# Wave 0's v loaded by GpSimd with the cast on the way, instead of by SyncE in float32

## The chip, the core and the metric

The kernel runs on one core of a Trainium2 chip. The core has a matrix engine (TensorE, "PE" in the profile), a vector engine (VectorE, "DVE"), a scalar engine (ScalarE, "ACT"), a general engine (GpSimd, "POOL") and a queue engine (SyncE, "SP"). Each runs its own instructions in order, and they wait for one another by semaphores. Transfers from and to device memory (DMAs) are issued by SP, ACT or POOL and carried out by 16 DMA engines that all of them share. The metric is the time of the whole program in device microseconds. Before the change it is 216.82 us, the median of 3 runs (216.48 to 217.40).

## What is computed

Two layers follow each other. The first is a linear attention with a decay per head, over 4 batches, 8 heads, 768 positions and 64 channels, block by block:

```python
intra = einsum('bhic,bhjc->bhij', qb, kb) * Dmask[None]
intra = einsum('bhij,bhjd->bhid', intra, vb)
inter = einsum('bhid,bhde->bhie', qb * lam_pow[None], kv_state)
out[:, :, sl] = intra + inter
kv_state = lam_block[None, :, None, None] * kv_state + einsum('bhsd,bhse->bhde', kb * rev_pow[None], vb)
```

Its result, seen as 3072 tokens of 512 channels, goes through an MLP with 2048 hidden units:

```python
h = x @ w_in
g = h * (1.0 / (1.0 + np.exp(-1.702 * h)))
return (g @ w_out).astype(np.float32)
```

All inputs and the output are float32; the kernel multiplies in bfloat16.

## The kernel before

The 768 positions are cut into 6 waves of 128 positions. A wave is all 4 batches and all 8 heads of its positions, so 512 tokens. The heads go in 4 pairs. For each wave and pair there is a tile of k, one of q and one of v, each of 128 positions x 4 batches x 2 heads x 64 channels. `load` (L78) fetches a tile by two DMAs, one for each head (L90), all from SP's queue; each moves 128 KB in 512 pieces of 256 bytes, since 64 float32 channels are all that lies together in memory.

The attention of a wave and pair goes through these steps. `cast_k` and `cast_q` (L176, L183) scale k and q by powers of the decay and write them as bfloat16. `cast_v` (L195) copies v as bfloat16 into `v_sb`, which holds for each batch the two heads with a block of zeros between them: [v of head 0, zeros, v of head 1]. `step_a` (L205) transposes k and q on TensorE, and VectorE copies the result out (L212). `step_s` (L220) multiplies k by q (L226), and VectorE applies the decay mask (L229, `sm`). `step_c` (L268) multiplies the masked scores by v (L280), and ScalarE writes the tokens `xT` (L283). `step_kv` (L233) makes the state for the next wave (L239), which in wave 0 ScalarE copies into `kv_sb` (L244).

The MLP of a wave follows: `mlp1` (L286) makes 16 chunks of hidden units from 4 chunks of tokens, ScalarE applies the activation (L296), and `mlp2` (L313) gives 4 output tiles. The order of instructions is written by hand. In wave 0, with which the program starts, the loop of L376 runs over the pairs, with filler matmuls (`keep_warm`, L328) between the steps, and the MLP of wave 0 begins when three pairs are done. From then on the attention of the next wave is woven into the MLP of this one.

SP's queue at the start holds, in this order, k and q of pairs 0 and 1, v of pair 0, k and q of pair 2, v of pair 1, k and q of pair 3, v of pair 2, then the first weight chunk `w_first` (512 KB, float32, L76), then v of pair 3. SP then waits for a weight chunk of `w_out` (L156), so that wave 1's loads stay behind the weights.

GpSimd sets up the identity, the index columns and the mask, clears the middle blocks of wave 0's `v_sb` (L367) and the first states (L369), casts v of pairs 0 and 1, and then waits for the last q (`pool_behind_loads`, L160) before it issues the weights of L144: `w_in_160`, `w_in_161`, `w_in_162`. These DMAs turn float32 into bfloat16 on the way. Behind them it casts the first half of `w_first` (L399), casts v of pair 3, and issues `w_in_163` and the four chunks of `w_out` (L149). ScalarE casts v of pair 2 and the other half of `w_first` (L400). The matmuls of the MLP start with that first chunk (`w_in_159` in the profile).

Of the kernel before, what the change touches and what calls it, by code (L numbers as in the profile page):

```python
# [24 lines left out]
def kernel(  # L25
# [13 lines left out]
    nc = tc.nc  # L39
# [3 lines left out]
    P = 128  # L43
    NP = H // 2
# [27 lines left out]
    loaded = {}  # L72

    def load_w_first():
        f = moe_w_in.rearrange("(kc ki) f -> ki kc f", ki=P)[:, :, 0 : IN_COLS[0] * P]
        nc.sync.dma_start(out=w_first, in_=f)  # L76

    def load(w, pairs=None, names="kqv"):  # L78

        if pairs is not None:  # L80
            order = [(nm, p) for p in pairs for nm in names]
        else:
            order = [x for p in range(NP) for x in [("k", p), ("q", p), ("v", p - 1)] if x[1] >= 0] + [("v", NP - 1)]
        for nm, p in order:
            if (w, nm, p) == (0, "v", NP - 1):
                load_w_first()
            x = ld.tile([P, B, 2, D], f32, tag=f"{nm}{p}", name=f"{nm}f")
            src = {"k": k, "q": q, "v": v}[nm]
            for h in range(2):
                nc.sync.dma_start(  # L90
                    out=x[:, :, h, :],
                    in_=src[:, 2 * p + h, w * P : (w + 1) * P, :].rearrange("b s d -> s b d"))
            loaded[nm, w, p] = x

# [39 lines left out]
    v_sb = [[const.tile([P, G, 3, D], bf16, name=f"v_sb{i}{p}") for p in range(NP)] for i in range(2)]  # L136
# [5 lines left out]
    def load_w_in(j):  # L142
        f0 = sum(IN_COLS[:j]) * P
        nc.gpsimd.dma_start(  # L144
            out=w_in_sb[j], in_=moe_w_in.rearrange("(kc ki) f -> ki kc f", ki=P)[:, :, f0 : f0 + IN_COLS[j] * P])

    def load_w_out():
        for j, x in enumerate(w_out_sb):
            nc.gpsimd.dma_start(  # L149
                out=x, in_=moe_w_out.rearrange("(fc fi) d -> fi fc d", fi=P)[:, j * CW : (j + 1) * CW, :])  # L150
# [3 lines left out]
    def sync_behind_weights():  # L154

        nc.sync.dma_start(out=behind, in_=w_out_sb[1][0:1, 0, 0:2])  # L156
# [3 lines left out]
    def pool_behind_loads():  # L160

        nc.gpsimd.tensor_copy(behind_q, loaded["q", 0, NP - 1][0:1, 0, 1, 0:1])
# [13 lines left out]
    def cast_k(w, p):  # L176
        kqs_of[w, p] = work.tile([P, 2, B, 2, D], bf16, tag=f"kqs{p}", name="kqs")
        f = loaded.pop(("k", w, p))
        for h in range(2):
            eng = (nc.gpsimd, nc.scalar)[h] if w == 1 else nc.vector  # L180
            scaled(eng, kqs_of[w, p], 0, f, p, h, k_pow)

    def cast_q(w, p):  # L183
        f = loaded.pop(("q", w, p))
        for h in range(2):
            eng = nc.scalar if w < 2 and not (w == 0 and p == NP - 1 and h == 1) else nc.vector
            scaled(eng, kqs_of[w, p], 1, f, p, h, q_pow)
        cast[w, p] = kqs_of[w, p].rearrange("p i b h d -> p i b (h d)")
        if w > 1:
            kq = work.tile([P, 2, B, P], bf16, tag=f"kq{p}", name="kqT")  # L190
            nc.sync.dma_start_transpose(out=kq.rearrange("p i b s -> p (i b) s"),
                                        in_=kqs_of[w, p].rearrange("p i b h d -> p (i b h d)"))
            trans[w, p] = kq

    def cast_v(w, p):  # L195
        copy = nc.scalar.copy if (w, p) == (0, NP - 2) else nc.gpsimd.tensor_copy
        copy(v_sb[w % 2][p][:, :, 0:3:2, :], loaded.pop(("v", w, p)))

    def do_cast(w, p):
        cast_k(w, p)  # L200
# [4 lines left out]
    def step_a(w, p):  # L205
        ps_t = ps.tile([P, 2, B, P], bf16, tag="s", bufs=4, name="ps_t")
        for i in range(2):
            for b in range(B):
                nc.tensor.transpose(ps_t[:, i, b, :], cast[w, p][:, i, b, :], ident)  # L209
        kq = work.tile([P, 2, B, P], bf16, tag=f"kq{p}", name="kq")  # L210
        for i in range(2):
            nc.vector.tensor_copy(kq[:, i], ps_t[:, i])  # L212
        trans[w, p] = kq
# [114 lines left out]
    def keep_warm(n):  # L328

        for _ in range(n):  # L330
            nc.tensor.matmul(warm_ps, ident, ident.rearrange("p (o s) -> p o s", o=1).to_broadcast([P, B, P]),  # L331
                             start=True, stop=True)
# [30 lines left out]
        return [(i - (14 if w == 2 else 20), x) for i, x in zip(at, steps)]  # L363

    with tc.manual_schedule():
        for p in range(NP):
            nc.gpsimd.memset(v_sb[0][p][:, :, 1, :], 0.0)  # L367
        for p in range(NP):
            nc.gpsimd.memset(kv_sb[1][p], 0.0)  # L369
        keep_warm(10)  # L370
        cast_k(0, 0)
        cast_q(0, 0)

        nc.scalar.activation(warm, q_pow[:, 0:1], GELU)
        step_a(0, 0)
        for p in range(1, NP):  # L376
            if p == NP - 1:
                pool_behind_loads()
                load_w_in(1)
                load_w_in(2)  # L380
                load_w_in(3)
            cast_k(0, p)
            cast_q(0, p)
            cast_v(0, p - 1)
            if p < NP - 1:
                keep_warm(2)
                step_s(0, p - 1)
                keep_warm(2)
                step_a(0, p)
                step_c(0, p - 1)  # L390
                step_kv(0, p - 1)
        p = NP - 1
        keep_warm(2)
        step_s(0, p - 1)
        keep_warm(2)
        step_a(0, p)
        keep_warm(2)
        step_c(0, p - 1)
        nc.gpsimd.tensor_copy(w_in_sb[0][:, :, 0:P], w_first[:, :, 0:P])  # L399
        nc.scalar.copy(w_in_sb[0][:, :, P : 2 * P], w_first[:, :, P : 2 * P])  # L400
        step_s(0, p)
        step_kv(0, p - 1)
        keep_warm(3)
        cast_v(0, NP - 1)
        load_w_in(4)
        load_w_out()
        sync_behind_weights()
        load(1)
        side, main = [(EARLY - 1, (step_c, 0, NP - 1)), (2 * EARLY, (step_kv, 0, NP - 1))], []
        for i in range(NP):  # L410
            side += [(4, (nc.gpsimd.memset, v_sb[1][i][:, :, 1, :], 0.0)), (4, (nc.gpsimd.memset, kv_sb[0][i], 0.0))]
        for w in range(NW):
            n = len(main)
            main += mlp_items(w)
            e = len(main)
            if w + 1 < NW:
                if w == 0:
                    m = EARLY + FFC
                    for at, f, p in ((9, cast_k, 0), (9, cast_q, 0), (11, step_a, 0), (11, cast_k, 1), (11, cast_q, 1),
                                     (11, cast_v, 0), (12, step_s, 0), (13, step_a, 1), (13, cast_k, 2),  # L420
                                     (13, cast_q, 2), (13, cast_v, 1), (14, step_kv, 0), (14, step_c, 0),
                                     (14, step_s, 1), (15, step_a, 2), (15, cast_k, 3), (15, cast_q, 3),
                                     (15, cast_v, 2), (15, cast_v, 3), (15, step_kv, 1), (15, step_c, 1),
                                     (15, step_s, 2), (16, step_a, 3), (16, step_kv, 2), (16, step_c, 2),
                                     (16, step_s, 3), (16 + EARLY - 1, step_c, 3), (16 + 2 * EARLY, step_kv, 3)):
                        side += [(m + at, (f, 1, p))]
                else:
                    for p in range(NP):
                        side += [(n + 1 + 2.0 * p, (do_cast, w + 1, p))]
                        if w == 1 and p < 2:  # L430
                            side += [(n + 1 + 2.0 * p, (load, 2, [p + 2], "kq"))]
                        elif w == 1:
                            side += [(n - 1 + 2.0 * p, (load, 2, [2 * p - 4, 2 * p - 3], "v"))]
                            side += [(n + 7 + p, (cast_v, 2, i)) for i in (2 * p - 4, 2 * p - 3)]
                    side += [(e + i, s) for i, s in attn_steps(w + 1)]
            if w == 0:
                side += [(EARLY + FFC + 3 * (FFC // CW), (load, 2, [0, 1], "kq"))]
            elif w + 2 < NW:
                side += [(n + 8 + 3 * p, (load, w + 2, [p])) for p in range(NP)]
        side.sort(key=lambda x: x[0])  # L440
        for i, (f, *a) in enumerate(main):
            while side and side[0][0] <= i:
                _, (g, *b) = side.pop(0)
                g(*b)
            f(*a)
# [30 lines left out]
```

## Time and profile before

| What | Value |
|---|---|
| Median of 3 runs | 216.82 us (216.48 to 217.40) |
| The profiled execution's own time | 216.82 us |
| Its span, first to last instruction | 215.1 us |
| TensorE busy | 206.1 us (96%) |
| VectorE, ScalarE, GpSimd busy | 89.6, 89.0, 33.4 us |
| TensorE clock granted | 0.997 |
| First MLP matmul starts | 19.99 us |

The profile is of one execution. Its times count from the first instruction; 1.7 us of the measured time lie outside the span. "SPq" and "POOLq" are instructions that only issue a DMA; the transfer itself shows as the time from issue to landing. "PEld" is TensorE's weight load, which runs beside the matmuls. An entry such as "19.99 1.47 PE L293 MATMUL ... x6 [0.75 <-POOL w_in_159 L399]" means: six matmuls of line 293 begin at 19.99 us and fill 1.47 us, and before them the engine sat idle for 0.75 us until GpSimd had written `w_in_159`. The buffers of `v_sb` for wave 0 are `v_sb_143` to `v_sb_146`, those of `kv_sb` for wave 1 `kv_155` to `kv_158`.

### The profile page before, as it was taken

How to read it: one execution, taken by the hardware profiler on the slowest of the kernel's cores; microseconds unless marked ns; L12 is line 12 of the kernel's file. 1: busy time of each engine (PE TensorE's matmuls, PEld its weight loads, DVE VectorE, ACT ScalarE, POOL GpSimd, SP SyncE). 2: the span in 40 equal slices, each digit the busy share in tenths (PEclk: the TensorE clock that was granted, in tenths of full speed). 3: DMA queues.
4: the chain of work that ended last, by engine and by line, in shares of the span. 5: the costliest groups of instructions: out<-in, count | busy, mean ns of one | idle time of the engine just before them, and what ended most of it. 6: DMA issues, size and time to landing. Idle time of an engine off the chain costs nothing.

```text
span 215.1 us, 3747 instructions
## 1 busy us (share of the span) xinstructions
PE 206.1 (96%) x1435; PEld 105.1 (49%) x1435; DVE 89.6 (42%) x193; ACT 89.0 (41%) x160; POOL 33.4 (16%) x65
## 2 busy tenths in 40 slices
PE   7687999999899999999999999999999999999993
PEld 2344444457544465545555445555445545444453
DVE  0775000079835348575173655274645061100121
ACT  5674864265277221166511176411266411466000
POOL 7126910234000222140111000121000000000000
PEclk9999999999999999999999999999999999999998
DMA  5999999999999999999899499899393114100112
GB/s 125 221 222 234 201 207 206 213 223 265 226 211 197 182 205 225 224 278 199 184 216 223 151 167 203 180 182 249 118 173 50 24 52 138 57 0 0 52 49 98
DMA packets 108117, 35.64 MB, mean 166 GB/s; under 512 B 100164, under 2 KB 105156, under 8 KB 108100
## 3 DMA queue, kind: packets, MB, share of 16 engines
q1 hardware_dynamic: 103732, 31.47, 69.5%
q0 software_dynamic: 4224, 3.93, 11.3%
q8 instruction: 11, 0.18, 0.4%
q14 instruction: 6, 0.05, 0.1%
q10 hardware_dynamic: 144, 0.00, 0.0%
HBM read 27.27 MB, written 6.29 MB: 156 GB/s over the span
## 4 chain that ended last, share of the span: by engine, by line
PE 85%; SPq 5%; DVE 4%; DMA 3%; issue 1%; POOL 0%; DVEq 0%
PE ps_h L293 38%; PE ps_out L318 36%; SPq L90 5%; DMA w_first<-in_moe_w_in_dram 3%; PE ps_s L226 2%; DVE sm L229 2%; PE ps_out L305 2%; PE ps_kv L239 2%; PE ps_o L260 1%; PE ps_o L280 1%; PE ps_o L258 1%; PE ps_o L278 0%; DVE kv_151 L246 0%; DVE kv_152 L246 0%; PE ps_t L209 0%
## 5 line engine op out<-in xcount | busy, mean ns | idle before, releaser
L296 ACT ACTIVATE g_sb<-ps_h 128x512 bf16<-128x512 f32 x96 | 56.8, 597 | 44.4 <-PE ps_h L293 44.1
L318 PEld LDWEIGHTS <-g_sb 128*128 128x128 bf16 x368 | 34.0, 98 | 36.5
L322 DVE COPY o_sb<-ps_out 128x512 f32<-128x512 f32 x21 | 14.5, 690 | 67.0 <-PE ps_out L318 66.8
L229 DVE SCALAR_TENSOR_TENSOR sm<-ps_s,inv_pow,mask 128x512 bf16<-128x512 f32 x48 | 33.1, 744 | 21.9 <-PE ps_s L226 21.7
L318 PE MATMUL ps_out<-w_out_167,g_sb 128*128 128x512 bf16 x92 | 23.5, 380 | 0.0
L318 PE MATMUL ps_out<-w_out_166,g_sb 128*128 128x512 bf16 x92 | 23.3, 380 | 0.0
L318 PE MATMUL ps_out<-w_out_164,g_sb 128*128 128x512 bf16 x92 | 23.3, 380 | 0.0
L318 PE MATMUL ps_out<-w_out_165,g_sb 128*128 128x512 bf16 x92 | 23.3, 379 | 0.0
L293 PE MATMUL ps_h<-xT,w_in_162 128*128 128x512 bf16 x96 | 22.7, 380 | 0.0
L293 PE MATMUL ps_h<-xT,w_in_163 128*128 128x512 bf16 x96 | 22.0, 379 | 0.0
L293 PE MATMUL ps_h<-xT,w_in_161 128*128 128x512 bf16 x96 | 21.7, 380 | 0.0
L263 ACT CAST x_tok<-ps_o 128x512 bf16<-128x512 f32 x12 | 7.0, 583 | 27.9 <-PE ps_o L260 27.9
L283 ACT CAST xT<-ps_o 128x512 bf16<-128x512 f32 x12 | 7.0, 585 | 24.9 <-PE ps_o L280 24.9
L172 DVE TENSOR_SCALAR kqs<-kf,k_pow 128x256 bf16<-128x256 f32 x40 | 12.6, 350 | 9.6 <-ACT k_pow L121 5.4
L293 PEld LDWEIGHTS <-w_in_161 128*128 128x128 bf16 x96 | 9.4, 98 | 11.3
L293 PEld LDWEIGHTS <-w_in_163 128*128 128x128 bf16 x96 | 9.3, 98 | 10.9
L293 PEld LDWEIGHTS <-w_in_162 128*128 128x128 bf16 x96 | 8.9, 98 | 10.2
L293 PE MATMUL ps_h<-xT,w_in_159 128*128 128x512 bf16 x48 | 11.7, 380 | 0.8 <-POOL w_in_159 L399 0.8
L293 PE MATMUL ps_h<-xT,w_in_160 128*128 128x512 bf16 x48 | 12.0, 379 | 0.1
L172 DVE TENSOR_SCALAR kqs<-qf,q_pow 128x256 bf16<-128x256 f32 x33 | 10.5, 350 | 2.5 <-DMA qf<-in_q_dram 2.3
L331 PE MATMUL ps_warm<-ident 128*128 128x512 bf16 x27 | 9.4, 473 | 1.5 <-POOL ident masks.py:199 1.5
L293 PEld LDWEIGHTS <-w_in_159 128*128 128x128 bf16 x48 | 4.5, 98 | 6.9 <-POOL w_in_159 L399 1.2
(147 smaller groups left out, 179.8 us busy)
## 6 DMA issues: line engine op xcount, KB each, us to landing
kf<-in_k_dram SPq DMA_DIRECT2D x48, 128.0 KB, 3.5
qf<-in_q_dram SPq DMA_DIRECT2D x48, 128.0 KB, 3.5
vf<-in_v_dram SPq DMA_DIRECT2D x48, 128.0 KB, 3.6
out_dram<-o_sb SPq DMA_DIRECT2D x23, 256.0 KB, 3.0
w_first<-in_moe_w_in_dram SPq DMA_DIRECT2D x1, 512.0 KB, 5.9
w_in_161<-in_moe_w_in_dram POOLq DMA_DIRECT2D x1, 512.0 KB, 7.6
w_in_162<-in_moe_w_in_dram POOLq DMA_DIRECT2D x1, 512.0 KB, 9.5
w_in_163<-in_moe_w_in_dram POOLq DMA_DIRECT2D x1, 512.0 KB, 8.4
```

The costliest lines, as they stand in the source:

```text
L90: nc.sync.dma_start(out=x[:, :, h, :], in_=src[:, 2 * p + h, w * P : (w + 1) * P, :].rearrange("b s d -> s b d"))
L172: eng.tensor_scalar(x[:, i, :, h, :], f[:, :, h, :], scalar1=pw[:, hd : hd + 1], scalar2=None, op0=MUL)
L226: nc.tensor.matmul(s2[h][:, b, :], kq[hs, 0, b, :], kq[hs, 1, b, :], start=True, stop=True)
L229: nc.vector.scalar_tensor_tensor(sm, s2[h], inv_pow[:, 2 * p + h : 2 * p + h + 1], mask.to_broadcast([P, B, P]), op0=MUL, op1=MUL)
L239: nc.tensor.matmul(ps_kv[:, b, :], ks[:, b, :], vt[:, b, 0:3:2, :], start=True, stop=True)
L263: nc.scalar.copy(xt, ps_o.rearrange("p b s -> p (b s)"))
L283: nc.scalar.copy(x, ps_o.rearrange("p b s -> p (b s)"))
L293: nc.tensor.matmul(h_ps[fc], w_in_sb[j][:, kc, i * P : (i + 1) * P], xT[w, kc], start=(kc == 0), stop=(kc == KC - 1))
L296: nc.scalar.activation(g_of[w][:, fc, :], h_ps.pop(fc), GELU)
L318: nc.tensor.matmul(ps_out, g_of[w][:, fc, g * P : (g + 1) * P], w_out_sb[j][:, fc % CW, :], start=(fc == 0), stop=(fc == FFC - 1))
L322: (nc.scalar.copy if w == 0 and g % 2 else nc.vector.tensor_copy)(o, ps_out)
L331: nc.tensor.matmul(warm_ps, ident, ident.rearrange("p (o s) -> p o s", o=1).to_broadcast([P, B, P]), start=True, stop=True)
```

## The change

Wave 0's v is no longer loaded by SP. A new function, `load_v`, issues the same two DMAs for each pair from GpSimd, and they write bfloat16 straight into the two head blocks of `v_sb`. The four casts of wave 0's v, three on GpSimd and one on ScalarE, are left out. GpSimd issues v of pairs 0 and 1 ahead of the clearing of the middle blocks, and v of pairs 2 and 3 between that and the clearing of the states. On SP's queue `w_first` now follows q of pair 3. All other waves are as they were.

```diff
@@ load @@
         for nm, p in order:
-            if (w, nm, p) == (0, "v", NP - 1):
-                load_w_first()
+            if (w, nm) == (0, "v"):
+                continue
             x = ld.tile([P, B, 2, D], f32, tag=f"{nm}{p}", name=f"{nm}f")
...
             loaded[nm, w, p] = x
+        if w == 0:
+            load_w_first()
+
+    def load_v(w, p):
+
+        for h in range(2):
+            nc.gpsimd.dma_start(
+                out=v_sb[w % 2][p][:, :, 2 * h, :],
+                in_=v[:, 2 * p + h, w * P : (w + 1) * P, :].rearrange("b s d -> s b d"))
@@ cast_v @@
-        copy = nc.scalar.copy if (w, p) == (0, NP - 2) else nc.gpsimd.tensor_copy
-        copy(v_sb[w % 2][p][:, :, 0:3:2, :], loaded.pop(("v", w, p)))
+        nc.gpsimd.tensor_copy(v_sb[w % 2][p][:, :, 0:3:2, :], loaded.pop(("v", w, p)))
@@ the order by hand @@
     with tc.manual_schedule():
+        load_v(0, 0)
+        load_v(0, 1)
         for p in range(NP):
             nc.gpsimd.memset(v_sb[0][p][:, :, 1, :], 0.0)
+        load_v(0, 2)
+        load_v(0, 3)
         for p in range(NP):
             nc.gpsimd.memset(kv_sb[1][p], 0.0)
...
             cast_k(0, p)
             cast_q(0, p)
-            cast_v(0, p - 1)
...
         keep_warm(3)
-        cast_v(0, NP - 1)
         load_w_in(4)
```

## The prediction

> **What bounds the kernel now.** I read the page's chain first, then TensorE's waits, then the timeline of the first 22 us, then the rates of the DMA engines by stretch.
>
> ```profile
> PE 85%; SPq 5%; DVE 4%; DMA 3%; issue 1%; POOL 0%; DVEq 0%
> ...
> PE ps_h L293 38%; PE ps_out L318 36%; SPq L90 5%; DMA w_first<-in_moe_w_in_dram 3%; PE ps_s L226 2%; DVE sm L229 2%; PE ps_out L305 2%; PE ps_kv L239 2%; PE ps_o L260 1%; PE ps_o L280 1%; PE ps_o L258 1%; PE ps_o L278 0%; DVE kv_151 L246 0%; DVE kv_152 L246 0%; PE ps_t L209 0%
> ```
>
> From 20 us on the chain is TensorE, without a gap that matters: its waits after 22 us sum to 0.6 us. Before that, the chain is SP's issuing and the landing of `w_first`. So whatever brings the first MLP matmul forward is won to the end, if nothing else becomes late.
>
> ```profile
> 13.37 0.54 SPq L76 DMA_DIRECT2D w_first<-in_moe_w_in_dram  x1
> ...
> 15.47 0.36 DVE L172 TENSOR_SCALAR kqs<-qf,q_pow 128x256 bf16<-128x256 f32 x1 [0.65 <-DMA qf<-in_q_dram]
> 15.50 0.18 POOL L162 COPY behind_q<-qf 1x1 f32<-1x1 f32 x1 [1.80 <-DMA qf<-in_q_dram]
> ...
> 15.62 0.98 POOL L144 DMA_DIRECT2D w_in_160<-in_moe_w_in_dram  x1
> ...
> 16.62 0.62 ACT L197 CAST v_sb_145<-vf 128x512 bf16<-128x512 f32 x1 [0.43 <-DMA vf<-in_v_dram]
> 17.07 0.74 DVE L212 COPY kq<-ps_t 128x512 bf16<-128x512 bf16 x2
> ...
> 17.86 0.40 PE L226 MATMUL ps_s<-kq 64*128 64x128 bf16 x8
> ...
> 18.43 0.81 PE L331 MATMUL ps_warm<-ident 128*128 128x512 bf16 x3
> ...
> 19.33 0.61 POOL L399 CAST w_in_159<-w_first 128x512 bf16<-128x512 f32 x1 [1.23 <-DMA w_first<-in_moe_w_in_dram]
> ...
> 19.99 1.47 PE L293 MATMUL ps_h<-xT,w_in_159 128*128 128x512 bf16 x6 [0.75 <-POOL w_in_159 L399]
> ```
>
> Two things hold up the MLP. The last attention step and fillers end at 19.24. Then 0.75 us pass until `w_first`, issued 13.37 and landed 5.9 us later, is cast. The attention itself is late because q of pair 3 lands only at 15.47.
>
> **What leaves SP's queue.** Eight DMAs at about 0.55 us (13.66 us for 24 of them and `w_first`). k and q of pair 2 move from 6.26 to 5.16, k of pair 3 from 9.71 to 7.39, q from 11.02 to 8.55, `w_first` from 13.37 to 9.71. By issue alone q of pair 3 would land 2.4 us earlier, at 13.1, and `w_first` at 15.6.
>
> **What the earlier q is worth.** Pairs 0 and 1 have their loads in time already, and VectorE and ScalarE set the pace between loads, so I followed the chain with the durations of the timeline. VectorE's mask of pair 0 ends at 10.0 as before. `step_c` of pair 0 follows at 10.06 instead of 10.22, since v no longer waits for a GpSimd cast (0.61). ScalarE's order (`xT` 0.58, state copies 0.76, q casts 0.91) carries these 0.16 us to the copy of pair 2, 13.38 to 14.14, and the cast of k of pair 3 ends at 14.66. There VectorE now wants q of pair 3, which it got at 15.47. `step_c` of pair 1, which waited for v until 13.76, goes at 13.34. The mask of pair 2 then runs 15.05 to 16.45 instead of 15.75 to 17.15, the copy of pair 3 to 17.11, `step_s` of pair 3 at 17.16 instead of 17.86, and the fillers end at 18.54 instead of 19.24. That is 0.70. ScalarE's cast of v (0.62) is gone and not missed. If `w_first` has landed by 17.85, the wait of 0.75 goes too: the MLP starts at 18.54, 1.45 us earlier. That is the most this change can give.
>
> **What the v costs on GpSimd.** Eight issues with 512 pieces each. The nearest rows are the weight issues, also 512 pieces: 0.98 for the first, 0.75 after. They start at 1.75, where a clearing stood; with one affine_select (0.28), four clearings (about 0.26 apart) and the rest at 0.75 the last ends near 9.4, the first state is cleared by 9.9, and ScalarE wants it at about 11.1. Cover: 1.2 us; beyond that each us delays ScalarE's state copies and so the q casts. `pool_behind_loads` waits for q anyway. GpSimd's three casts (1.83) are gone. `w_in_160` to `w_in_162` keep their place behind q of pair 3, and the cast of `w_first` behind them is reached 1.6 us after q lands.
>
> [...] If the six k casts up to 11.2 (0.35 each) all blocked an issue, the last would end 2 us later, near 11.4, and the state copy would be up to 0.8 late; I leave it out of the sum.
>
> **What the v costs on the DMA engines.** This decides. The 16 engines look full, but the rate says that it is SP's issue that they follow.
>
> ```profile
> core 0: us, PE busy (x) PEld busy (x) DVE busy (x) ACT busy (x) POOL busy (x), PEclk, DMA share, GB/s
> 10.00:14.00 4.00, 3.01 (x37) 1.91 (x38) 3.05 (x8) 2.12 (x5) 0.78 (x2) 1.00 1.36 218
> 95.75:96.75 1.00, 1.00 (x7) 0.41 (x5) 0.00 (x0) 0.64 (x2) 0.00 (x0) 1.00 1.28 268
> 24.00:36.00 12.00, 12.00 (x58) 5.44 (x56) 0.00 (x0) 8.82 (x17) 3.62 (x9) 1.00 1.24 205
> ```
>
> The same 256-byte packets go at 218 GB/s here and at 268 behind a stall, where a backlog drains. The landings of the front come exactly 0.60 us apart; on one engine with a backlog (18.78 to 19.68) packets started every 14.1 ns, so that its 32 packets of a DMA take 0.45 us. A quarter of each engine is free. GpSimd's casting DMAs write 205 GB/s, so read 410; by bytes read, no more than the other queue's packets.
>
> So for v I take 14.1 ns a packet, 0.45 us a DMA, 3.6 us in all on each engine. The bounds: 10 ns (an eighth of the 83 ns per packet that the 2.65 us between the landings of `w_in_160` and `w_in_161` give), and 41 ns (half of it, were the cost mostly per packet). 14.1 is the row of the same size. First data come 2.25 us after an issue (15.62 to 17.87 for `w_in_160`), for v from 4.07. From there both queues keep the engines busy: 14 DMAs of k and q at 0.45 (6.3) and v (3.6), and a landing about 0.7 after the last packet. So q of pair 3 lands at 4.07 + 6.3 + 3.6 + 0.7 = 14.7, where VectorE wants it at 14.66. `w_first`, 1.5 us behind, lands near 16.3, in time. On the way q of pair 1 (landed 8.3, wanted 8.63 for its second head) comes at about 9.2: some 0.2 us at the copy of pair 1, most of which its slack takes. v of pair 0 lands near 6, wanted at 10.0. No loss excludes a gain here, and below 14.1 nothing more is won.
>
> [...]
>
> **What becomes late next.** The weights. `w_in_161` lands at 24.2, TensorE first uses it at 24.29: no slack. It is issued behind q of pair 3, so moves 0.8 earlier where the matmuls move 1.45. It landed late because one engine was held up for 1.7 us at 15.78 (one packet of `w_first`); 13 of the 16 engines had it 1.5 us sooner. I allow 0.25 us for this and for q of pair 1 together. Wave 1's loads wait for `w_out` and move with it; the cast of `w_first` (GpSimd free at 16.3) is no wait.
>
> **Sum.** 0.75 + 0.70 - 0.25 = 1.2 us, from an execution of 216.82 (span 215.1), which equals the median: 215.6.
>
> **Rivals.** (1) *The engines are shared, and the gain goes there.* If the engine that was held up at 15.78, 0.16 us after GpSimd's first issue, was held up by that first issue, the same happens near 2 us: k and q of the first pairs are 1.3 late on it, q of pair 1 by 1.1 beyond its slack, and the chain follows: 1.45 - 1.1 = 0.35, time 216.5. The same comes of 18 ns a packet with the weights late. For it: the coincidence; against: one packet of one engine. (2) *Slower: v's packets are dear.* At x ns a packet v costs 0.256 x us. q of pair 3 may land at 16.1 before the MLP starts no earlier than now (14.66 + 1.45), which is x = 20. At 24 ns it lands at 17.1 and the MLP starts at 21.0: 217.8; at 41 ns, 222. For it: casting packets lasted 60 and 98 ns where plain ones of the same bytes read lasted 46 and 84; against: the rate by bytes. (3) *v makes no difference because VectorE is the pace*: then only the 0.75 go, 216.1.
>
> **How the numbers follow.** A measurement tells about 0.5%, 1.1 us, from no change. Forecast (215.2 to 216.0) 0.50, of which 0.10 falls within 0.5%; rivals 1 and 3 together 0.25, nearly all within 0.5%; rival 2 0.25, of which 0.20 is beyond 0.5%. Faster 0.40, same 0.38, slower 0.22 (0.02 of rivals 1 and 3). The range leaves out the dearest part of rival 2 and a little below: 215.0 to 218.4.
>
> **What would show it.** Right: q of pair 3 lands by 15.0 and VectorE does not wait for it long; no wait of TensorE for `w_in_159`; the first MLP matmul near 18.7; no wait for `w_in_161`; v's landing 3 to 4 us after issue. Wrong: landings of k and q 5 us or more after issue, a wait of ScalarE for q of pair 1, SP's issues stretched, v issues over 1 us, or a new wait on line L301.

## The result and the profile after

The changed kernel is slower. Its median is 219.93 us (4 runs, 219.33 to 220.23) against 216.69 us of the kernel before on the same chip: a ratio of 1.014, 95% interval 1.0108 to 1.0172. The prediction was 215.6 us. The profiled execution took 220.23 us, with a span of 218.4 us (215.1 before) and a granted TensorE clock of 0.984 (0.997 before).

The end of the page's chain, by engine and by line, for the changed kernel:

```profile
PE 82%; DMA 6%; SPq 5%; DVE 4%; issue 1%; POOL 0%; DVEq 0%
PE ps_h L301 36%; PE ps_out L326 36%; SPq L90 5%; DMA w_in_149<-in_moe_w_in_dram 4%; PE ps_s L234 2%; DMA qf<-in_q_dram 2%; DVE sm L237 2%; PE ps_out L313 2%; PE ps_kv L247 1%; PE ps_o L268 1%; PE ps_o L266 1%; PE ps_o L288 1%; PE ps_o L286 0%; DVE kv_139 L254 0%; DVE kv_140 L254 0%
```

`w_first` has left the chain, as the change intended. In its place stand q (`qf`) and the second of GpSimd's weight chunks, `w_in_149` (called `w_in_161` before). The same chain for the first 30 us alone, in order of time (start, length, what):

```profile
12.76 4.32 DMA qf<-in_q_dram
17.08 0.05 issue
17.14 0.18 POOL behind_q L171
17.31 0.06 issue
17.37 0.73 POOL w_in_148 L153
18.11 9.47 DMA w_in_149<-in_moe_w_in_dram
27.58 0.04 issue
27.62 2.55 PE ps_h L301 x11
```

Read it upwards from TensorE. At 27.62 TensorE gets `w_in_149`, which it had at 24.50 before: 3.1 us, nearly the whole loss (the spans differ by 3.3). This chunk was issued at 18.11, because GpSimd issues the weights behind the landing of the last q, and the last q landed at 17.08. Before, it landed at 15.44.

The waits of the first 30 us show what else is new (engine, what waits, for what; us in total, times, longest):

```profile
POOL behind_q L171 <- DMA qf<-in_q_dram: 6.0, 1, 6.0
PE ps_t L217 <- DVE kqs L181: 3.0, 2, 2.5
ACT kqs L179 <- DMA qf<-in_q_dram: 1.8, 3, 0.8
PE ps_h L301 <- DMA w_in_149<-in_moe_w_in_dram: 1.1, 1, 1.1
```

TensorE waits 2.5 us at once for VectorE's first casts of k. The timeline of the changed kernel shows them beside GpSimd's work:

```profile
5.21 0.35 POOL L377 MEMSET v_sb_131<- 128x256 bf16 x1
5.42 2.43 DVE L181 TENSOR_SCALAR kqs<-kf,k_pow 128x256 bf16<-128x256 f32 x2 [5.42 <-ACT k_pow L130]
6.22 1.51 POOL L100 DMA_DIRECT2D v_sb_133<-in_v_dram  x2
7.91 0.76 PE L217 MATMUL ps_t<-ident,kqs 128*128 128x128 bf16 x8 [2.46 <-DVE kqs L181]
9.15 0.60 POOL L381 MEMSET kv_143<- 128x512 bf16 x1
9.38 2.17 DVE L181 TENSOR_SCALAR kqs<-kf,k_pow 128x256 bf16<-128x256 f32 x2
10.55 0.60 POOL L381 MEMSET kv_146<- 128x512 bf16 x1
```

The same two casts in the kernel before, where GpSimd was done with its clearing at 4.93 us:

```profile
5.42 0.62 DVE L172 TENSOR_SCALAR kqs<-kf,k_pow 128x256 bf16<-128x256 f32 x2 [5.42 <-ACT k_pow L121]
```

The operation is the same, and it took 2.43 us in place of 0.62, while GpSimd cleared and issued DMAs. The MLP's first matmul starts at 21.84 us in place of 19.99.

### The profile page after: what moved, and what is told of

Its sections match the earlier page's. It is cut to its first block, busy times and chain, and to the rows that moved or that the text cites. A ratio compares the mean times of both kernels' runs of the same rounds, so it can differ in the third digit from the quotient of the medians.

```text
span 218.4 us, 3737 instructions
## 1 busy us (share of the span) xinstructions
PE 208.1 (95%) x1435; PEld 106.4 (49%) x1435; DVE 92.8 (43%) x193; ACT 88.7 (41%) x159; POOL 38.0 (17%) x70
## 4 chain that ended last, share of the span: by engine, by line
PE 82%; DMA 6%; SPq 5%; DVE 4%; issue 1%; POOL 0%; DVEq 0%
PE ps_h L301 36%; PE ps_out L326 36%; SPq L90 5%; DMA w_in_149<-in_moe_w_in_dram 4%; PE ps_s L234 2%; DMA qf<-in_q_dram 2%; DVE sm L237 2%; PE ps_out L313 2%; PE ps_kv L247 1%; PE ps_o L268 1%; PE ps_o L266 1%; PE ps_o L288 1%; PE ps_o L286 0%; DVE kv_139 L254 0%; DVE kv_140 L254 0%
## 5 line engine op out<-in xcount | busy, mean ns | idle before, releaser
L330 DVE COPY o_sb<-ps_out 128x512 f32<-128x512 f32 x21 | 14.5, 690 | 67.4 <-PE ps_out L326 67.2
L237 DVE SCALAR_TENSOR_TENSOR sm<-ps_s,inv_pow,mask 128x512 bf16<-128x512 f32 x48 | 33.1, 745 | 22.7 <-PE ps_s L234 22.6
L301 PE MATMUL ps_h<-xT,w_in_149 128*128 128x512 bf16 x96 | 21.7, 379 | 1.1 <-DMA w_in_149<-in_moe_w_in_dram 1.1
L301 PE MATMUL ps_h<-xT,w_in_150 128*128 128x512 bf16 x96 | 22.7, 379 | 0.0
L301 PE MATMUL ps_h<-xT,w_in_151 128*128 128x512 bf16 x96 | 22.0, 379 | 0.0
L181 DVE TENSOR_SCALAR kqs<-kf,k_pow 128x256 bf16<-128x256 f32 x40 | 16.0, 435 | 9.9 <-ACT k_pow L130 5.4
L301 PEld LDWEIGHTS <-w_in_149 128*128 128x128 bf16 x96 | 9.3, 98 | 12.7 <-DMA w_in_149<-in_moe_w_in_dram 1.6
L301 PEld LDWEIGHTS <-w_in_151 128*128 128x128 bf16 x96 | 9.3, 98 | 10.8
L301 PEld LDWEIGHTS <-w_in_150 128*128 128x128 bf16 x96 | 8.9, 98 | 10.2
L301 PE MATMUL ps_h<-xT,w_in_148 128*128 128x512 bf16 x48 | 12.0, 379 | 0.1
L339 PE MATMUL ps_warm<-ident 128*128 128x512 bf16 x27 | 10.3, 508 | 1.5 <-POOL ident masks.py:199 1.5
L301 PE MATMUL ps_h<-xT,w_in_147 128*128 128x512 bf16 x48 | 11.7, 379 | 0.1
L217 PE MATMUL ps_t<-ident,kqs 128*128 128x128 bf16 x64 | 5.7, 234 | 3.1 <-DVE kqs L181 3.0
```

Of the source, the lines that this page charges most:

```text
L181: eng.tensor_scalar(x[:, i, :, h, :], f[:, :, h, :], scalar1=pw[:, hd : hd + 1], scalar2=None, op0=MUL)
L237: nc.vector.scalar_tensor_tensor(sm, s2[h], inv_pow[:, 2 * p + h : 2 * p + h + 1], mask.to_broadcast([P, B, P]), op0=MUL, op1=MUL)
L301: nc.tensor.matmul(h_ps[fc], w_in_sb[j][:, kc, i * P : (i + 1) * P], xT[w, kc], start=(kc == 0), stop=(kc == KC - 1))
L330: (nc.scalar.copy if w == 0 and g % 2 else nc.vector.tensor_copy)(o, ps_out)
```

## The experiments

**Three theories.** (A) GpSimd holds up VectorE's casts: the clears, which stood before 5 us, and the new DMA issues now run until 11 us. (B) The two DMA queues share the 16 engines, so that v takes time from k and q. (C) The clock: TensorE's 2.5 us gap is followed by a stretch of lower granted clock (0.53 in 8 to 12 us, 0.62 in 12 to 16), which makes it slow where it should catch up.

**e1: the changed kernel with the eight clearings on VectorE.**

```diff
+            nc.vector.memset(v_sb[0][p][:, :, 1, :], 0.0)
...
+            nc.vector.memset(kv_sb[1][p], 0.0)
+        for p in range(NP):
+            load_v(0, p)
```

> The changed kernel with its eight clearings (middle blocks of v_sb, first states) moved from GpSimd to VectorE, before VectorE's first cast; GpSimd issues the eight v DMAs back to back from 1.75 us. Theory lock (GpSimd's work keeps VectorE's casts of k waiting: 1.69, 0.82 and 1.91 us where 0.35 is usual): the casts that met clearings fall back to 0.35; if the DMA issues hold them too, the first two still take 1 us or more. Time 218 to 219. Theory queues (v's packets share the 16 DMA engines with k and q, and q of pair 3 therefore lands at 17.1): landings as in the changed kernel, time 219.5 to 220.

Three of its four executions lie at 219.21 to 219.62 us, ratio 1.0112 (1.0076 to 1.0147). The gain over the changed kernel, 0.3%, is within the intervals: by its time this run decides nothing on (A). The profiled execution took 754 us and is left out of the comparison: TensorE was busy for 748 us of it, for a reason that is not known, while VectorE and GpSimd were busy for 92.7 and 33.1 us, as in the other kernels. So only what does not wait for TensorE can be read in its trace. Its first two casts of k meet DMA issues on GpSimd (until 8.20) and no clears:

```profile
5.44 0.91 DVE L181 TENSOR_SCALAR kqs<-kf,k_pow 128x256 bf16<-128x256 f32 x2 [2.87 <-ACT k_pow L130]
```

They took 0.91 us, and a later pair, with GpSimd idle, 0.61. So issues alone stretched a pair by 0.3 us in this one trace, and with the clears gone 1.5 of the 2.43 us were gone too. The last q landed at 16.92 even so.

**e2: the kernel before with eight more clearings on GpSimd**, of a scratch tile that nothing reads. No DMA is touched.

```diff
+        for p in range(8):
+            nc.gpsimd.memset(scratch, 0.0)
```

> The kernel before with eight more clearings of a scratch tile on GpSimd, behind the first states, so that GpSimd is busy from 4.9 to about 8.7 us; no DMA is changed. Theory lock: VectorE's casts of k at 5.4 and 7.9 take 1 us or more, the first transposes come 1 to 2 us later, and the time rises to 217.5 to 218.5. Theory queues: casts stay at 0.35 and the time at 216.7.

The timeline of e2:

```profile
4.89 4.69 POOL L372 MEMSET scratch<- 128x512 bf16 x8
5.45 1.28 DVE L173 TENSOR_SCALAR kqs<-kf,k_pow 128x256 bf16<-128x256 f32 x2 [5.45 <-ACT k_pow L121]
8.12 0.99 DVE L173 TENSOR_SCALAR kqs<-kf,k_pow 128x256 bf16<-128x256 f32 x2
11.01 0.60 DVE L173 TENSOR_SCALAR kqs<-kf,k_pow 128x256 bf16<-128x256 f32 x2
```

Clears alone do it: the pairs of casts that run beside them take 1.28 and 0.99 us, and the pair after they have ended 0.60. So the effect that (A) supposes is shown without any change of the loads. Its price here is nothing, where the theory had asked for 0.8 us or more: 216.89 us, ratio 0.9994 (0.9967 to 1.0021). The first transposes come 0.70 us later, and the chain, which waits for loads, takes that in. What lets GpSimd's clears hold up a cast no run here shows.

This kernel showed one thing more. Its MLP started at 19.03, 0.96 earlier than before, because `w_first` landed at 18.11 in its profile, and it still ended with the same span, 215.1. The step of attention behind it then waited for v of pair 3. So in the kernel before the wait of 0.75 us for `w_first` had another wait close behind it.

**e3: the changed kernel with wave 0's casts of k written as an operation with two tensor inputs** (the second is a tile of ones; the result is the same). That a cast of this form would not be held up was the author's guess; no run before had shown it.

```diff
+        elif i == 0 and eng is nc.vector and wave == 0:
+            eng.scalar_tensor_tensor(x[:, i, :, h, :], f[:, :, h, :], pw[:, hd : hd + 1],
+                                     ones.to_broadcast([P, B, D]), op0=MUL, op1=MUL)
```

> [...] Theory lock: all eight casts take 0.4 to 0.5 us, the first transposes start near 6.2 instead of 7.9, and the time falls to 218 to 219. Theory queues: the time stays at 219.5 to 220, since the landings of q set the chain.

The timeline of e3 at the same place as above:

```profile
5.45 0.88 DVE L181 SCALAR_TENSOR_TENSOR kqs<-kf,k_pow,ones 128x256 bf16<-128x256 f32 x2 [4.46 <-ACT k_pow L130]
6.22 2.99 POOL L100 DMA_DIRECT2D v_sb<-in_v_dram  x4
8.33 0.87 DVE L181 SCALAR_TENSOR_TENSOR kqs<-kf,k_pow,ones 128x256 bf16<-128x256 f32 x2
```

Beside the same GpSimd work the casts now take 0.48 each, the MLP starts at 20.64 in place of 21.84, and the time is 218.63 us, ratio 1.0079 (1.0040 to 1.0118). Why the second input frees them no run shows. So (A) is worth 1.2 us at the start of the MLP. What it is worth in time this run does not say alone: in its profile the second weight chunk also landed early, at 24.11, 6.2 us after its issue, where the changed kernel's took 9.5. And the last q still landed at 16.89, and the kernel is still slower than before: (A) is not all.

**e4: the changed kernel with twenty filler matmuls at the start in place of ten.**

```diff
-        keep_warm(10)
+        keep_warm(20)
```

> The changed kernel with 20 instead of 10 filler matmuls at the start, which fill TensorE's gap from 5.45 to 7.9 us. Theory clock (the gap makes the granted clock fall to half from 8.5 to 15.4 us, and TensorE's steps at half speed delay the front): the clock stays full and the time falls by 0.5 to 1 us, to about 219. Theory lock or queues alone: TensorE is not the pace of the front, the time stays within 0.3 of 219.9.

220.14 us, ratio 1.0142 (1.0108 to 1.0177): no gain. The windows of e4 (stretch and its length, busy time of each engine, granted clock, DMA share, GB/s):

```profile
8.00:12.00 4.00, 2.29 (x26) 1.29 (x26) 3.43 (x5) 1.54 (x4) 3.15 (x6) 0.99 1.77 198
12.00:16.00 4.00, 3.61 (x31) 2.28 (x29) 2.48 (x7) 2.08 (x5) 0.00 (x0) 0.59 1.46 212
```

The clock held 4 us longer (0.99 to 12 us, where the changed kernel had 0.53 from 8 on) and nothing was won, so the low clock before 12 us is not what costs. The stretch from 12 to 16 us this run does not speak on; n7 below does.

**n0 and n1: both kernels without DMA transposes.** In both kernels SP transposes tiles by DMA in waves 2 to 5, and TensorE's waits for these differ from profile to profile (1.2 us in all in e4's, 0.7 in e3's, none listed in those of the kernels before and after). From here on TensorE transposes in all waves (`step_a`, which waves 0 and 1 use already), and all waves make their tokens with `step_c`, as waves 0 to 2 do; the front is untouched. These kernels are slower, so they are compared with n0, their own base. Each also has a ratio to the kernel before on the same chip, and where they ran in another group the ratios are compared.

```diff
-            nc.sync.dma_start_transpose(out=kq.rearrange("p i b s -> p (i b) s"),
...
+                        side += [(n + (9 if w == 1 else 5) + 2.0 * p, (step_a, w + 1, p))]
```

> The kernel before, with waves 2 to 5 transposed on TensorE, as waves 0 and 1 are, in place of by DMA: the base for the runs beside it. The front up to the first MLP matmul is untouched, so all theories expect its MLP to start at 20.0 us as before. TensorE gets 4 x 32 more transposes of k and q and loses none: about 128 of some 60 to 110 ns, so 225 to 235 us in all.

> The change on that base. If the loss is made in the front alone (shared queues and blocked casts), the MLP starts at 21.8 us as in the changed kernel and the time is 1.5 to 2.0 us over the base's. If something behind the front adds to it (the rival: DMA transposes of later waves that come late and hold up TensorE), the changed kernel's full 3.2 us is not seen here, since they are gone: both read on the start of the MLP and on the difference of the two times. Over 3 us here would say that neither the DMA transposes nor the front alone make it.

n0: 227.95 us, ratio 1.0491 (1.0464 to 1.0519). n1: 230.57 us, ratio 1.0599 (1.0566 to 1.0633). The difference, 2.6 us or 1.1%, lies between the 2.0 and the 3.0 that the expectation named: what is left of the 3.2 us for the later DMA transposes, 0.6, is within the intervals. The front makes 2.6, more than the 1.5 to 2.0 that was expected of it, and in n1's profile it is made before the MLP, which starts at 22.66 (19.33 in n0). Its TensorE waits of the first 30 us:

```profile
PE ps_t L211 <- DVE kqs L180: 2.8, 2, 2.0
PE ps_warm L312 <- POOL ident masks.py:199: 1.5, 1, 1.5
PE ps_s L228 <- DVE kq L214: 0.4, 1, 0.4
PE ps_o L261 <- DVE sm L231: 0.2, 1, 0.2
```

Here TensorE is so late that no weight chunk is waited for. In the changed kernel it was 0.8 us less late and waited 1.1 for the chunk. The sum is nearly the same, which hints at two bounds that cover each other.

**n5: n1 with the two-input casts of e3**, to take one of them away.

> The changed kernel on the TensorE-transpose base (230.57 us; its base 227.95) with the casts of k in wave 0 as operations with two tensor inputs, which GpSimd did not hold up. Its chain goes through the held-up casts and VectorE's queue behind them, and not through q. Theory: 1.2 us of the 2.6 go, 229.0 to 229.8, and the rest is q's late landing. Rival (all of it is the casts): 228.2 or less. Rival (the casts only hide q's landing): over 230.

229.91 us, ratio 1.0579 (1.0549 to 1.0609). The MLP starts at 20.49, 2.2 us before n1's, but of that gain only 0.2% or 0.4 us arrived by the ratios, which the intervals do not even separate from none. That is less than the 1.2 us of the theory, and nearest to the second rival, that the casts only hide q's landing. Two waits of n5's TensorE are not in n1's list, one for ScalarE's casts of q and one for the weights:

```profile
PE ps_t L216 <- ACT kqs L178: 2.7, 2, 1.4
PE ps_h L279 <- DMA w_in<-in_moe_w_in_dram: 1.4, 1, 1.4
```

The second weight chunk landed at 26.30 (24.03 in n0), since the last q, behind which it is issued, landed at 16.65 (15.46).

**n8 and n9: the weights alone, moved by as much.** n8 is n0 with its weights issued behind v of pair 2 (landed 16.59) in place of q of pair 3. n9 is n5 with its weights issued behind k of pair 3 in place of q of pair 3.

```diff
-        nc.gpsimd.tensor_copy(behind_q, loaded["q", 0, NP - 1][0:1, 0, 1, 0:1])
+        nc.gpsimd.tensor_copy(behind_q, loaded["v", 0, NP - 2][0:1, 0, 1, 0:1])
```

> The TensorE-transpose base (227.95 us) with its weights issued behind the landing of v of pair 2 (16.6 us) in place of q of pair 3 (15.5 us), nothing else. Theory (the weight stream behind q is a second bound, the second chunk lands at 24.0 us and TensorE is ready for it at 24.4): 1.1 us later eats the slack of 0.3, so 0.5 to 1.1 us slower, 228.4 to 229.1, with a wait of TensorE for w_in. Rival (the weights have room, and the wait in the two-input kernel was one late transfer): 227.7 to 228.2.

> The changed kernel with two-input casts on the TensorE-transpose base (229.91 us) with its weights issued behind the landing of k of pair 3 (15.5 us) in place of q of pair 3 (16.65 us). Theory (the weights are the second bound): TensorE's wait for the second chunk goes from 1.4 us to 0.3 or less and the time to 228.7 to 229.4. Rival (the weights' packets share the engines with q of pair 3 and make it later by as much): 229.7 or more.

n8: 229.51 us, ratio 1.0551 (1.0520 to 1.0582), so 0.6% or 1.3 us over n0, with nothing else changed. A wait of its TensorE after 20 us, and its chain from 12.85 us until TensorE goes on:

```profile
PE ps_h L266 <- DMA w_in<-in_moe_w_in_dram: 2.1, 1, 2.1
```

```profile
12.85 3.74 DMA vf<-in_v_dram
16.59 0.05 issue
16.64 0.18 POOL behind_q L161
16.82 0.91 POOL w_in L143
17.73 8.87 DMA w_in<-in_moe_w_in_dram
26.60 0.05 issue
```

It is the chain of the changed kernel, made by 1.1 us of delay of the weights alone. The chunk landed 2.6 us later than in n0, since its transfer, too, took longer (8.9 us in place of 7.4). The price of 1.3 us is above the 1.1 that the theory allowed, though not by more than the intervals.

The profile of n8 is of the slowest of its seven executions, 232.05 us; the other six took 229.18 to 229.94. In it the granted clock fell behind the wait, in wave 0's MLP (windows with the columns of e4's; n0 had 1.00 in both):

```profile
24.00:28.00 4.00, 1.94 (x7) 0.62 (x6) 0.00 (x0) 1.69 (x5) 2.99 (x9) 0.81 1.23 201
28.00:32.00 4.00, 4.00 (x16) 1.62 (x15) 0.00 (x0) 1.89 (x4) 0.00 (x0) 0.76 1.24 205
```

So the 2.1 us of wait need not be those of the median. Of the extra 2.5 us of this execution the lower clock is worth up to 1.7, by an estimate from these windows (0.19 and 0.24 of 4 us each; from 28 to 32 us TensorE was busy for all 4.00).

n9 is the reverse: 229.33 us, ratio 1.0546 (1.0519 to 1.0574), 0.3% below n5, and TensorE no longer waits for a weight chunk, though its MLP started later than n5's (21.19). The last q landed at 16.90, 0.25 later than in n5: the earlier weights did not take from it what they gave. So the weights behind q are a second bound of this front. n8 shows it by its time, just outside the intervals; n9 shows it by the wait that is gone, while its 0.3% alone is no more than the intervals.

**n4: n5 without the cast on the way.** v goes through GpSimd's queue as float32, and GpSimd casts it afterwards.

> The changed kernel on the TensorE-transpose base with two-input casts of k, where v goes through the GpSimd queue as float32 and GpSimd casts it afterwards. Theory (the queues' packets take turns, whatever is done to the data on the way): as many packets of the same read size, so the last q lands at about 16.9 us as in the kernel with two-input casts, and v's packets take turns at the same rate. Rival (the cast on the way makes v's packets dear): the last q lands at 14.7 to 15.9 us.

The last q landed at 18.06, later than with the cast (16.53 in n1, 16.65 in n5), so the rival's forecast, that q comes earlier without the cast, falls. (One run, 231.29 us.) The theory was off too, by 1.2 us: it took the packets to be as many and as large as before, and they are not. The DMA queues from 4 to 13 us (queue: packets, MB, share of 16 engines), first the kernel before, then the changed kernel, then n4:

```profile
q1 hardware_dynamic: 8028, 1.99, 131.6%
```

```profile
q0 software_dynamic: 4152, 0.52, 89.8%
q1 hardware_dynamic: 4921, 1.22, 75.5%
```

```profile
q1 hardware_dynamic: 4365, 1.08, 76.2%
q0 software_dynamic: 339, 0.93, 46.4%
```

q1 is SP's queue, q0 GpSimd's. In 9 us SP's queue moved 8028 packets when it was alone, 892 a us. Beside v it moved 4921, 547 a us, and v 4152, 461 a us (each reads 256 bytes and writes 128). Together that is 1008 a us, 13% more than SP alone. The prediction's 14.1 ns a packet on each of 16 engines is 1135 a us. In n4 v's packets hold up to 4096 bytes and are few, but the bytes come out alike: 1.08 MB of k and q, 0.93 of v, 2.01 together, which is what SP's queue did alone (1.99). So in these two kernels the queues shared about equally by what they read (54% and 46% in both), and float32 in both moved no more than one queue did. What one packet of v costs by its cast n4 does not show, since it changed their size as well. By the shares above, a record of v lasts 31 ns in the changed kernel (0.898 x 16 x 9 us / 4152) and one of k and q 22, but the records overlap. That the queues take turns packet by packet, as the expectations suppose, was the author's guess: the shares near half and half fit it, but no run here shows a turn or its size.

**n2: n0 with v of pairs 0 and 1 alone through GpSimd's queue, clears on VectorE.** GpSimd is done with it at 5.2 us.

```diff
+        load_v(0, 0)
+        load_v(0, 1)
         for p in range(NP):
-            nc.gpsimd.memset(v_sb[0][p][:, :, 1, :], 0.0)
+            nc.vector.memset(v_sb[0][p][:, :, 1, :], 0.0)
```

> The base with v of pairs 0 and 1 alone through the GpSimd queue, issued from 1.75 us, clears on VectorE. Theory (the two queues' packets take turns one by one): 2048 packets of v on the GpSimd queue cost k and q 0.95 in place of 0.60 us a DMA for about four DMAs, 1.45 us; SP's queue is shorter by four DMAs, 2.4 us; so the last q lands at about 14.5 us (15.4 before, 17.1 after), VectorE's casts take 0.35 us each again, and the time is 1.0 us under to 0.2 over the base's. Rival (packets of the GpSimd queue are dear in themselves): the last q no earlier than 16 us, time over 1 us above the base's.

The front behaved as the theory said. The last q landed at 14.81 (expected 14.5; 15.46 in n0), and the casts are as in the kernel before, as the timeline of n2 shows:

```profile
5.81 0.62 DVE L181 TENSOR_SCALAR kqs<-kf,k_pow 128x256 bf16<-128x256 f32 x2 [3.24 <-ACT k_pow L130]
8.31 0.61 DVE L181 TENSOR_SCALAR kqs<-kf,k_pow 128x256 bf16<-128x256 f32 x2
```

The time did not: 228.84 us, ratio 1.0525 (1.0492 to 1.0558), 0.9 us above n0 where 1.0 below to 0.2 above was expected. Some 0.3 of this lies outside the span: 2.0 to 2.1 us in n2's runs, 1.7 in n0's, for a cause that is open. The MLP starts at 19.42, as n0's (19.33), for the chain of n2's first 26 us now goes through v of pair 3, the last load of SP's queue:

```profile
13.97 4.68 DMA vf<-in_v_dram
...
18.78 0.62 POOL v_sb L203
```

The profiled execution (228.05 us) is even with n0. Of the six runs three, at a granted clock of 0.998 to 1.0, took 228.05 to 228.60 us, and three, at 0.990 and 0.991, 229.09 to 229.52. Which of clock and delay is the cause of the other is not settled.

**n3: n0 with v of pair 3 alone through GpSimd's queue**, issued behind the loads and ahead of the weights.

```diff
+                load_v(0, 3)
                 load_w_in(1)
```

> The base with v of pair 3 alone moved to the GpSimd queue, behind the issue of the loads there and ahead of the weights. Theory: v of pair 3 is what the last attention step waits for once the wait for the weights is short; it lands earlier than 20.3 us and its cast is gone, so the step is up to 0.8 us earlier, and the time 0.1 to 0.9 us under the base's. Rival: the weights, issued 1.5 us later, come late: the time is up to 1 us over the base's.

229.97 us, ratio 1.0572 (1.0540 to 1.0603), 2.0 us above n0: the rival, at twice its price. TensorE's waits in the first 30 us:

```profile
PE ps_h L278 <- DMA w_in<-in_moe_w_in_dram: 1.3, 1, 1.3
PE ps_h L278 <- POOL w_in L385: 1.2, 1, 1.2
```

Two issues ahead of the weights make the issue of the second chunk 1.5 us later and its landing 2.2 (26.22), and, behind them on GpSimd, the cast of `w_first` comes later too.

**n6 and n7: n2 and n0 without the ten filler matmuls between the pairs**, n7 being the control.

```diff
-                keep_warm(2)
                 step_s(0, p - 1)
-                keep_warm(2)
                 step_a(0, p)
```

> v of pairs 0 and 1 through the GpSimd queue with clears on VectorE (228.84 us; 228.05 where the clock held), without the ten filler matmuls between the pairs. If TensorE's own queue or the late v of pair 3 sets the start of the MLP: without fillers TensorE waits for v of pair 3 all the same, so 227.5 to 228.3. Rival (the clock falls in the gaps without fillers): the front runs at half clock, 229 to 231.

> The base (227.95 us) without the same ten filler matmuls: the control for the run beside it. The loads set its MLP start, so the fillers are beside the path: 227.5 to 228.2 if the clock holds, 229 to 231 if it falls.

n6: 229.16 us, ratio 1.0582 (1.0533 to 1.0631), no faster than n2, where 227.5 to 228.3 was expected if the clock did not matter; two of its six runs, both at a clock of 0.968, took 231.2 and 231.5. n7: 227.84 us, ratio 1.0492 (1.0463 to 1.0522), the same as n0. The windows of n7, with the columns of e4's:

```profile
8.00:12.00 4.00, 2.91 (x36) 2.20 (x35) 3.17 (x9) 1.75 (x6) 0.61 (x1) 0.71 1.39 218
12.00:16.00 4.00, 3.24 (x35) 2.39 (x32) 3.04 (x7) 2.37 (x7) 1.06 (x3) 0.50 1.33 223
```

The clock was at half for much of the front, as in the changed kernel, and the MLP still started at 19.60 and the time did not move. With the loads in time, and ten matmuls fewer for TensorE, half the clock in this stretch cost nothing. The changed kernel's own runs say the same: one had a mean granted clock of 1.000 and took 219.94 us, one had 0.982 and took 219.91. Together with e4 this leaves no support for (C) as a cause of its own. In n8's profiled execution, where the low clock (0.81 and 0.76) fell into the MLP, it went with a time 2.5 us over the median, in that one trace.

None of these versions is faster than the kernel before.

## Why the prediction was wrong, point by point

**The step that failed first: "From there both queues keep the engines busy", and q "at 4.07 + 6.3 + 3.6 + 0.7 = 14.7".** The last q landed at 17.08. The packets of k, q and v, 9.9 us in that sum, took 12.3 (17.08 - 4.07 - 0.7); v's first packet started at 3.65, which makes it 12.7. The reading under it was that the landings 0.60 us apart follow SP's issue, that "a quarter of each engine is free", and that a DMA could go in 0.45. That 0.45 came from one engine that caught up behind a stall; all 16 with both queues did not keep this pace. Beside GpSimd's queue the gain was 13%, and SP's queue fell from 892 to 547 packets a us. And without v it was no faster either: v's last DMA landed at 14.27, and then the last five of k and q, issued 4.3 to 6.3 us before they landed and so with work waiting in the queue, came 0.48 to 0.60 us apart. So the 0.45 did not come back with work waiting, and SP's issue was not the pace. The trace of before had a sign of it: SP's issues took about 0.55 us each, and the time from issue to landing grew from 3.3 to 3.9 us along the queue. By what was measured, q landed 4.0 us behind the 13.1 that SP's issue alone gave, where the prediction had 1.6.

**Rival 2, v's packets dear, gave the right landing, but no run shows its reason.** At 24 ns a packet it had q at 17.1, the measured value, and the MLP at 21.0 with 217.8 us. Taking the cast away (n4) made q later still, so the cast alone is not the reason; what the runs show is that the queues share. The agreement of the number is luck as far as that goes. And the time came out 2 us worse than this rival, by the next two points.

**What VectorE and GpSimd do to each other was weighed in one direction only.** The prediction asked what VectorE's casts would do to GpSimd's issues, put it at 2 us if each of six casts blocked one, and left it out of the sum. The issues did take 0.98 and then 0.75, and the last ended at 9.22 (9.4 predicted). The harm went the other way: behind the issues GpSimd's clears moved from 1.75 to 4.93 us to between 5.21 and 11.15, into VectorE's casts, and two casts cost 2.43 us, then 2.17, in place of 0.62. The trace of before could not show it, since there GpSimd was done before VectorE began. That was the place for a bound from both sides, which the prediction gave only for GpSimd.

**"What becomes late next. The weights" was the right mechanism with the wrong sign.** No slack at `w_in_161`, and its issue tied to q of pair 3: both hold, and n8 shows the price. The prediction let the weights move 0.8 earlier with an earlier q and allowed 0.25; q came 1.6 later, and the chunk 3.1 later, at 27.58. The extra comes from the chunk itself: 7.6 us from issue to landing before, 9.5 after. Nor was an earlier start of the MLP "won to the end": in e2 it started 0.96 us earlier with the loads as they were, and the span stayed at 215.1.

**Right:** the wait for `w_first` is gone. Nearly all signs named for a wrong prediction appeared: k and q landed a median of 5.1 and 5.5 us after issue, ScalarE waited for q of pair 1 (0.78), pairs of SP's issues were stretched to 2 us and more, and L301 had a new wait. Only the v issues stayed under 1 us. The range, to 218.4, ended below the result; it would have had to hold rival 2 and the two other costs together.

**How the loss divides.** On the base without DMA transposes, by ratios against n0: the changed kernel is 1.0% over; with the casts freed it is 0.8%; with the weights earlier as well, 0.5%. Each step is within the width of the intervals, the sum of both is just outside them. What is left, 0.5%, fits q's later landing, since TensorE of n9 waits 2.5 us in all for ScalarE's casts of q (0.5 in n0). It was not taken away by itself in a run, and the two-input casts, 0.13 us longer each, may have a part in it.

## What to carry to other kernels

Moving DMAs to another engine's queue took eight issues off SP here, and the transfers that stayed with SP became late: SP's queue fell from 892 to 547 packets a us, and the last q landed at 17.08 us in place of 15.44. So count both queues at a common rate measured with both running (here 1008 packets a us). Then follow every wait that is tied to the landing that moves, here weights issued behind the last q: they carried its delay past the stage that was looked at, and TensorE got the second chunk 3.1 us later. And when an engine's instructions move in time, look at what runs on the other engines in the new place, in both directions: here two casts took 2.43 us in place of 0.62.

## What the runs showed of the hardware that was not expected

- GpSimd's clears alone stretched a pair of VectorE casts of 128x256 from float32 to bfloat16 with one tensor input to 1.28 us in e2, where the pair took 0.62 (one cast 0.35) in the kernel before; beside clears and DMA issues a pair took up to 2.43 in the changed kernel, beside issues alone 0.91 (one trace, e1). The same cast with a second tensor input took 0.48 in e3 and was not held up: in n5 a pair took 0.88 beside GpSimd's work and 0.87 with GpSimd idle.
- Two queues of 256-byte reads, one with the cast to bfloat16, moved 1008 packets a us together in the changed kernel, where one moved 892 before; both in float32 (n4, one run), 2.01 MB in 9 us, where one moved 1.99. SP's queue alone landed a 128 KB DMA each 0.60 us before the change, and, with five of them waiting, one each 0.48 to 0.60 us after v was done in the changed kernel.
- The second weight chunk (512 KB) finished on the 16 engines at very different times: between the first and the last engine's part lay 0.9 us in e3, 2.1 before, 4.1 in the changed kernel. It bears on how much of q's delay the weights pass on; its cause stays open.
- A granted clock of 0.71 in 8 to 12 us and 0.50 in 12 to 16 cost no time in n7 (227.84 us; 227.95 in n0 at 1.00 in both). In n8's profiled execution the low clock fell into the MLP (0.81 in 24 to 28 us, 0.76 in 28 to 32), and that execution took 2.5 us more than n8's median.
